# Gated linear attention and a cosine-gated MLP on one core: pairs 0 and 1 take both parities' decays from TensorE, and every engine gets a new written order

## The chip, the cores and the metric

The kernel runs on one core of one Trainium2 chip. The metric is the device time of one execution in microseconds (us), the median of several. Engines are named as the profile names them: PE is TensorE's matmul, PEld its weight load, DVE VectorE, ACT ScalarE, POOL GpSimd, and SP SyncE, which here only issues DMAs. A line such as L479 is a line of the kernel file; the changed file is longer, so its lines have other numbers.

## The reference

```python
B, H, S, D = 4, 8, 768, 48
f = 1.0 / (1.0 + np.exp(-f_logit))
for t in range(S):
    state = f[:, :, t, :, None] * state + np.einsum('bhd,bhe->bhde', k[:, :, t], v[:, :, t])
    y[:, :, t] = np.einsum('bhd,bhde->bhe', q[:, :, t], state)
x = y.transpose(0, 2, 1, 3).reshape(B * S, H * D)      # 3072 x 384
h = x @ w_in                                           # 3072 x 2048
out = (h * np.cos(h)) @ w_out                          # 3072 x 384, float32
```

The recurrence runs along the sequence, for each of 32 (batch, head) pairs with its own 48x48 state; the MLP then takes all heads of a token together.

## The kernel before

**Tiling.** A *pair* is 256 tokens of one batch, two chunks (g = 0, 1) of 128 tokens with all eight heads; there are 12 pairs, three to a batch. In a pair a partition holds an even and an odd token (parity e = 0, 1). The MLP works on *units* of 256 tokens, unit m on pair m's result.

**Steps of pair n** (u = 0, 1 is a half of four heads; pairs 0 and 1 are loaded and decayed by halves, `cut`, the others whole):

- `f`, `k`, `q`, `v`: loads on SP's queue (L296), 384 KB each, 192 KB for a half. `w0.i`, `w1.i` (L282): four parts each of `w_in` and `w_out`, 768 KB a part, into slots of the pool `g`; `wc0.i`, `wc1.i` (L197) cast a part to bf16 on POOL or ACT.
- `ex`, `ln` (L329, L333, ACT): the softplus of -f_logit, which is minus the log of the gate. `ad` (L363, POOL) adds both parities. `cum` (L374, L380, PE): products with a triangular matrix sum the logs over the tokens. `eb`, `ei` (L391, L395, ACT): exp of minus and plus that sum, the tiles `b` and `bi`.
- `fx`, `fy` (L347, L344), `ka` (L351), `qa` (L341; L338 in cut pairs) bring the one parity from the other: k's even token is multiplied by the odd token's gate, q's by its inverse. `qm`, `km` (L404, POOL or DVE): q times `b` and k times `bi`.
- `tq`, `tk` turn q and k: on PE (L435) with a copy `qkt` out of PSUM in pairs 0 to 3, by a DMA transpose (L424) in pairs 4 to 11. `sc` (L456, PE) and `am` (L461, DVE): scores and their mask. `vb`, `vt` (L197): casts and copies of v.
- `ps` (L479, PE): the state's increment. `st` (L497, DVE) adds the carried state to it in PSUM, `sz` (L503, DVE) decays the sum. `y`, `yi` (L531, PE): the output from within the pair and from the carried state; `xe` (L197) copies it out as the MLP's input.

**Steps of unit m**: eight `h` (L579, PE, six matmuls of 256 columns each), four `co` (L584, ACT, cosine), four `g` (L561, DVE), then for each of its two blocks of 128 tokens (numbered 0 to 23) four `o` (L595, PE, four matmuls of 384 columns), `ot` (L197) and the store `out` (L606). Part i of `w_out` is read by the steps `o*.i`.

**Order.** The text `ORDER` lists every step with its engine and its slots (`w0.1:Y0` is step w0.1 on SP, slot 0; T is PE, S ACT, V DVE, G POOL). It is all that sets each engine's instruction order; an engine takes its instructions strictly one behind the other, and a wait holds up all behind it. `zf` are fillers: products of zeros (L264, 512 columns) that nobody reads, placed where PE would wait. Each core fetches its instructions from memory by DMA as well: the profile counts them as queues of kind "instruction".

## Time and profile before

| | us |
|---|---|
| median of 3 runs (181.22 to 182.77) | 181.72 |
| span of the profiled execution, first to last instruction | 179.3 |
| PE busy in it | 171.0 (95%) |
| of that the 50 recorded fillers | 14.8 |
| DVE / ACT / POOL busy | 137.8 / 131.3 / 109.2 |
| the three DMA kinds: data loads and stores, share of 16 engines | 81.4% |

The profile gives no time of its own for the profiled execution beside its span. The 2.4 us between span and median lie around the span, before the first and behind the last instruction. A row of the timeline reads: start, duration, engine, line, operation, what it writes and reads, sizes, count, and in brackets the engine's idle time ahead of it with what ended it. In the table of stages the columns behind each stretch are its length, the busy time of PE, PEld, DVE, ACT and POOL, TensorE's granted clock, the DMA engines' busy share (over 1 where packets overlap) and GB/s.

### The profile page before, as it was taken

What the parts mean: (1) busy time and instruction counts of PE and PEld (TensorE: products, weight loads), DVE (VectorE), ACT (ScalarE), POOL (GpSimd) and SP (SyncE); (2) the same over time, 40 slices, a digit from 0 to 9 for tenths busy, and PEclk for the clock granted to TensorE, in tenths of its full rate; (3) what the DMA queues carried; (4) which work ended last, traced back from release to release, by engine and by line L of the source; (5) the groups of instructions that cost most, each with busy time, mean ns of one, the idle gap of its engine ahead of it and who ended that gap; (6) DMA issues with size and microseconds to landing.
All of it is one profiled execution on the core that took longest, in us unless ns stands there. A gap on an engine that the chain in (4) does not pass through costs nothing.

```text
span 179.3 us, 5727 instructions
## 1 busy us (share of the span) xinstructions
PE 171.0 (95%) x2412; PEld 122.9 (69%) x2414; DVE 137.8 (77%) x206; ACT 131.3 (73%) x185; POOL 109.2 (61%) x139
## 2 busy tenths in 40 slices
PE   7998899999999999999999998999999999999992
PEld 2453568876578866778668885668877766867761
DVE  6379998998894989969899887768689996385330
ACT  3899878886999998988999979858973702364410
POOL 7498699976979998789977295827992000000000
PEclk9999999999999999999999999999999999999999
DMA  6999999999999799999999999959045900004013
GB/s 156 262 261 287 356 324 315 306 274 328 257 257 236 168 190 180 282 277 198 249 203 262 226 254 207 234 131 268 4 106 121 148 0 4 4 0 176 0 50 129
DMA packets 74394, 34.46 MB, mean 192 GB/s; under 512 B 67456, under 2 KB 72832, under 8 KB 74368
## 3 DMA queue, kind: packets, MB, share of 16 engines
q1 hardware_dynamic: 73696, 33.79, 81.4%
q8 instruction: 19, 0.31, 0.8%
q10 hardware_dynamic: 672, 0.30, 0.6%
q14 instruction: 7, 0.06, 0.1%
HBM read 25.17 MB, written 4.72 MB: 167 GB/s over the span
## 4 chain that ended last, share of the span: by engine, by line
PE 69%; DMA 10%; POOL 7%; SPq 5%; DVE 5%; issue 3%; ACT 0%; POOLq 0%; DVEq 0%; ACTq 0%
PE ps L595 29%; PE ps L579 29%; DMA q<-in_q_dram 7%; SPq L296 5%; PE ps L531 4%; DMA qkt<-qk 3%; PE ps L456 3%; POOL qk L404 3%; PE ps L479 1%; POOL sp L363 1%; PE ps L435 1%; DVE qk L404 1%; POOL vt L197 1%; DVE sz L503 1%; PE ps L374 1%
## 5 line engine op out<-in xcount | busy, mean ns | idle before, releaser
L561 DVE TENSOR_TENSOR g<-ps,co 128x1024 bf16<-128x1024 f32 x48 | 57.7, 1221 | 15.3 <-ACT co L584 11.3
L595 PE MATMUL ps<-w_out_bf,g 128*128 128x384 bf16 x384 | 68.4, 326 | 0.0
L579 PE MATMUL ps<-x,w_in_bf 128*128 128x256 bf16 x576 | 66.7, 273 | 0.4 <-issue 0.4
L584 ACT ACTIVATE co<-ps,halfpi 128x1024 bf16<-128x1024 f32 x48 | 52.6, 1115 | 17.7 <-PE ps L579 14.4
L579 PEld LDWEIGHTS <-w_in_bf 128*128 128x128 bf16 x576 | 55.8, 98 | 9.2 <-issue 0.6
L595 PEld LDWEIGHTS <-g 128*128 128x128 bf16 x384 | 36.0, 98 | 21.5
L461 DVE TENSOR_TENSOR am<-ps,pmask 128x1024 bf16<-128x1024 f32 x24 | 28.7, 1215 | 3.6 <-PE ps L456 3.5
L404 POOL TENSOR_TENSOR qk<-q,b 128x384 bf16<-128x384 f32 x22 | 21.9, 1002 | 2.6 <-DVE q L338 1.7
L404 POOL TENSOR_TENSOR qk<-k,bi 128x384 bf16<-128x384 f32 x22 | 21.9, 1007 | 1.6 <-ACT bi L391 1.1
L197 POOL COPY vt<-vb 64x384 bf16<-64x384 bf16 x31 | 15.9, 514 | 1.4
L264 PE MATMUL ps<-zero 128*128 128x512 bf16 x50 | 14.8, 435 | 1.3 <-DVE zero L203 1.2
L503 DVE TENSOR_TENSOR sz<-ps,b 64x192 bf16<-64x192 f32 x40 | 14.2, 354 | 1.9 <-PE ps L479 0.9
L351 POOL TENSOR_TENSOR k<-k,f 128x384 f32<-128x384 f32 (+1 forms) x13 | 11.7, 904 | 6.2 <-DMA k<-in_k_dram 2.9
L197 DVE COPY ot<-ps 128x384 f32<-128x384 f32 (+1 forms) x17 | 8.7, 519 | 8.5 <-PE ps L595 6.0
L341 POOL TENSOR_TENSOR q<-f,q 128x384 f32<-128x384 f32 x10 | 10.0, 999 | 8.1 <-DMA q<-in_q_dram 8.1
L363 POOL TENSOR_TENSOR sp<-ls 128x384 bf16<-128x384 f32 x10 | 10.3, 1029 | 4.4 <-issue 2.2
L497 DVE TENSOR_TENSOR ps<-ps,sz 64x192 f32<-64x192 f32 x32 | 11.7, 366 | 1.4 <-PE ps L479 0.3
L329 ACT ACTIVATE f<-f 128x768 f32<-128x768 f32 (+1 forms) x14 | 10.4, 748 | 2.7 <-DMA f<-in_f_logit_dram 2.5
L197 ACT CAST x<-ps 128x384 bf16<-128x384 f32 x12 | 5.5, 479 | 8.6 <-PE ps L531 8.6
L197 ACT COPY ot<-ps 128x384 f32<-128x384 f32 (+1 forms) x9 | 4.1, 455 | 8.9 <-PE ps L595 8.9
L456 PE MATMUL ps<-qkt 48*64 48x128 bf16 (+1 forms) x320 | 8.6, 219 | 1.9 <-DVE qkt L197 1.0
L264 PEld LDWEIGHTS <-zero 128*128 128x128 bf16 x52 | 5.1, 108 | 6.9 <-issue 2.5
(61 smaller groups left out, 166.2 us busy)
## 6 DMA issues: line engine op xcount, KB each, us to landing
v<-in_v_dram SPq DMA_DIRECT2D x12, 384.0 KB, 6.1
out_dram<-ot SPq DMA_DIRECT2D x22, 192.0 KB, 2.8
f<-in_f_logit_dram SPq DMA_DIRECT2D x10, 384.0 KB, 5.6
k<-in_k_dram SPq DMA_DIRECT2D x10, 384.0 KB, 6.1
q<-in_q_dram SPq DMA_DIRECT2D x10, 384.0 KB, 6.4
g<-in_moe_w_in_dram SPq DMA_DIRECT2D x4, 768.0 KB, 7.5
g<-in_moe_w_out_dram SPq DMA_DIRECT2D x4, 768.0 KB, 7.2
k<-in_k_dram SPq DMA_DIRECT2D x4, 192.0 KB, 5.0
```

Source lines behind the costliest of these rows:

```text
L197: (nc.scalar.copy if e == "ACT" else eng(e).tensor_copy)(out=o, in_=i)
L264: G.step(f"zf{i}", ("PE",), lambda e, dump=dump: nc.tensor.matmul(dump.ap, lhsT=zero[:, 0:128], rhs=zero, start=True, stop=True), writes=[ ...
L351: eng(e).tensor_mul(out=w.ap[:, :, 0, :], in0=w.ap[:, :, 0, :], in1=t.ap[:, :, 0, :])
L363: G.step(f"ad{n}", ("POOL",), lambda e: eng(e).tensor_add(out=sp.ap[:, 0, :, 0:D], in0=soft.ap[:, :, 0, :], in1=soft.ap[:, :, 1, :]), read ...
L404: G.step(f"{nm}{n}.{u}", ("POOL", "DVE") if cut else ("POOL",), lambda e, u=u, j=j, src=src, dec=dec: eng(e).tensor_mul(out=qkp[u][j].ap[: ...
L456: nc.tensor.matmul(o[t0:t1, r, 2 * a + g, :].rearrange("p (e n) -> p e n", e=2), lhsT=wide[s, t0 // 64, :] if turned else wide[s].rearrang ...
L461: G.step(f"am{n}.{u}", ("DVE",), lambda e, u=u, sc=sc: nc.vector.tensor_mul(out=am[u].ap.rearrange("p r b n -> p (r b) n"), in0=sc.ap.rear ...
L503: eng(e).tensor_mul(out=new.ap[s, :, r, :].rearrange("p (u a) n -> p u a n", u=2), in0=view()[s].rearrange("p (u a) n -> p u a n", u=2), i ...
L561: nc.vector.tensor_mul(out=o.rearrange("p b (n e) -> p b n e", e=2), in0=ph.ap.rearrange("p (b e n) -> p b n e", e=2, n=64), in1=co.ap.rea ...
L579: nc.tensor.matmul(ph.ap[:, i * T:(i + 1) * T].rearrange("p (g t) -> p g t", t=C), lhsT=w_in_bf[:, kk, f0:f0 + 128], rhs=xa[:, :, kk, :], ...
L584: G.step(f"co{m}.{j}", ("ACT",), lambda e, ph=ph, co=co: nc.scalar.activation(out=co.ap, in_=ph.ap, func=AF.Sin, bias=halfpi), reads=[ph], ...
L595: nc.tensor.matmul(po.ap[:, 0:DM], lhsT=gT.ap[:, j, i * C:(i + 1) * C], rhs=w_out_bf[:, j, :], start=(po.first and j == 4 * s), stop=(po.f ...
```

## The change

In pairs 0 and 1 `cum` now makes one sum for each parity: a step has four products of 192 columns instead of two, three with the triangle that includes its own token and one with the strict one. `eb` and `ei` are twice as wide and go to new tiles `bb` and `bj`; `qm` and `km` take them for both parities at once. So `fx`, `qa` and `ka` of pairs 0 and 1 go. In pair 1 (`CARRY_PE`) the carried state is added by two products with the identity for each chunk (`si1.0`, `si1.1`, PE) behind the `ps` steps, and the four `st1` steps on DVE go. Fillers drop from 52 to 28. `ORDER` is new from end to end. The code for pairs in `VLIE` is not used, as `VLIE` is empty; it is left out here.

```diff
+CARRY_PE = (1,)
-ZEROS = 52
+ZEROS = 28
...
+    bbS = slots("bb", [128, 2, 2 * HB + 4], F32)
+    bjS = slots("bj", [128, 2, 2 * HB], F32)
...
-        sp, bt, bi = Val(spS), Val(bS), Val(biS)
+        sp, bt, bi = Val(spS), Val(bbS if cut else bS), Val(bjS if cut else biS)
...
+            if cut:
+                continue
             G.step(f"fx{n}{u}", ("ACT",), ...
...
+        W = HB * len(xe)
...
-            for x in xe:
-                nc.tensor.matmul(o[:, :, 0:HB], lhsT=incl,
-                                 rhs=w[:, x, :, 0:D].rearrange("p (u h) d -> p u h d", u=un),
-                                 start=(x == 0), stop=False)
+            for z in xe:
+                for x in xe:
+                    nc.tensor.matmul(o[:, :, HB * z:HB * z + HB], lhsT=strict if x > z and cut else incl,
+                                     rhs=w[:, x, :, 0:D].rearrange("p (u h) d -> p u h d", u=un),
+                                     start=(z == 0 and x == 0), stop=False)
...
-            if S0 is not None:
+            if S0 is not None and n in CARRY_PE:
+                def add(e, g=g, S0=S0):
+                    for r in range(2):
+                        nc.tensor.matmul(ps[g].ap[:, 0:HB].rearrange("p (a n) -> p a n", n=D), lhsT=ident,
+                                         rhs=S0.ap[:, :, r, :], start=(ps[g].first and r == 0),
+                                         stop=(ps[g].final and r == 1))
+                G.step(f"si{n}.{g}", ("PE",), add, reads=[S0] + both, writes=[ps[g]], sums=True)
+            elif S0 is not None:
...
-zvt.2:V zsp.2:V f0.1:Y0 zqk.2:G zsp.0:G f0.0:S ex0.1:S ln0.1:S2 f1.0:Y2 ex0.0:S fx0.1:S ln0.0:S
+f1.1:Y2 f0.1:S1 zf0:T5 v0:Y0 f0.0:S zf1:T0 q0.0:Y1 zqk.2:G k1.1:Y1 zqk.0:G zvt.2:G k0.0:Y2 ex1.1:S
```

**Three places in the order.** First the loads on SP behind the halves of q1, before: the four parts of `w_in` (`moe_w_in`, in the order 1, 0, 3, 2), pair 3's k and q, the parts 2, 0, 1, 3 of `w_out`, pair 2's q and k, pair 3's v.

```order
L282 DMA g_0_143<-in_moe_w_in_dram 128x3x512
L282 DMA g_1_144<-in_moe_w_in_dram 128x3x512
L296 DMA k_2_99<-in_k_dram 128x8x96
L282 DMA g_4_147<-in_moe_w_in_dram 128x3x512
L282 DMA g_0_143<-in_moe_w_in_dram 128x3x512
L296 DMA q_2_102<-in_q_dram 128x8x96
L282 DMA g_1_144<-in_moe_w_out_dram 128x4x384
L282 DMA g_4_147<-in_moe_w_out_dram 128x4x384
L296 DMA q_1_101<-in_q_dram 128x8x96
L296 DMA k_0_97<-in_k_dram 128x8x96
L296 DMA v_2_105<-in_v_dram 128x8x96
L282 DMA g_0_143<-in_moe_w_out_dram 128x4x384
```

And now the same stretch, with the parts of `w_in` in the order 1, 0, 2, 3 and pair 2's k and q apart:

```order
L295 DMA g_0_148<-in_moe_w_in_dram 128x3x512
L295 DMA g_3_151<-in_moe_w_in_dram 128x3x512
L295 DMA g_1_149<-in_moe_w_in_dram 128x3x512
L309 DMA k_2_100<-in_k_dram 128x8x96
L295 DMA g_2_150<-in_moe_w_in_dram 128x3x512
L309 DMA q_2_103<-in_q_dram 128x8x96
L295 DMA g_4_152<-in_moe_w_out_dram 128x4x384
L309 DMA k_1_99<-in_k_dram 128x8x96
L295 DMA g_3_151<-in_moe_w_out_dram 128x4x384
L309 DMA q_1_102<-in_q_dram 128x8x96
L309 DMA v_2_106<-in_v_dram 128x8x96
L295 DMA g_2_150<-in_moe_w_out_dram 128x4x384
```

No part of `w_in` goes to a slot that an earlier part holds any more (slot 0 stood twice before). Behind this the last part of `w_out`, which before stood ahead of pair 2's v, now stands behind it, as the last load ahead of pair 4's. 

Second, POOL from the first cast of `w_in` to the first of `w_out`, before (L351, L341, L404 are pair 3's `ka`, `qa` and its `km` and `qm`):

```order
L197 CAST w_in_bf<-g_143 128x3x512
L197 CAST w_in_bf<-g_144 128x3x512
L351 TENSOR_TENSOR k_99<-k_99,f_94 128x8x48
L404 TENSOR_TENSOR qk_119<-k_99,bi_115 128x8x48
L197 CAST w_in_bf<-g_147 128x3x512
L197 CAST w_in_bf<-g_143 128x3x512
L404 TENSOR_TENSOR qk_119<-k_99,bi_115 128x8x48
L341 TENSOR_TENSOR q_102<-f_94,q_102 128x8x48
L404 TENSOR_TENSOR qk_119<-q_102,b_112 128x8x48
L197 CAST w_out_bf<-g_144 128x1536
```

Now (L360, L350, L416 are the same three kinds):

```order
L196 CAST w_in_bf<-g_148 128x3x512
L196 COPY vt_130<-vb_122 64x8x48
L196 CAST w_in_bf<-g_149 128x3x512
L360 TENSOR_TENSOR k_100<-k_100,f_96 128x8x48
L416 TENSOR_TENSOR qk_120<-k_100,bi_115 128x8x48
L196 CAST w_in_bf<-g_150 128x3x512
L350 TENSOR_TENSOR q_103<-f_96,q_103 128x8x48
L416 TENSOR_TENSOR qk_120<-q_103,b_113 128x8x48
L416 TENSOR_TENSOR qk_120<-k_100,bi_115 128x8x48
L416 TENSOR_TENSOR qk_120<-q_103,b_113 128x8x48
L196 CAST w_out_bf<-g_152 128x1536
```

One cast of `w_in` has gone to ACT, and all four `qm` and `km` of pair 3 now stand ahead of the first cast of `w_out`, where three did.

Third, PE's start. Before, eleven fillers stood ahead of the first `cum`; now two do (each product has a weight load of its own ahead of it):

```order
L277 LDWEIGHTS zero
L277 MATMUL ps_165<-zero 128x512
L277 LDWEIGHTS zero
L277 MATMUL ps_163<-zero 128x512
L386 LDWEIGHTS incl
L386 MATMUL ps_164<-sp_109,incl 128x192
L386 LDWEIGHTS strict
L386 MATMUL ps_164<-sp_109,strict 128x192
L386 LDWEIGHTS incl
L386 MATMUL ps_164<-sp_109,incl 128x192
L386 LDWEIGHTS incl
L386 MATMUL ps_164<-sp_109,incl 128x192
```

L386 is `cum` of pair 1's second half, whose logits are now loaded first. In the text of `ORDER` the start-up on PE reads so (without slots): two fillers, `cum1.1`, four fillers, `cum0.0`, four, `cum0.1`, two, `tk0.0`, and on to `si1.0`, `tk1.0`, `yi0`, `y0`, `tq1.0`, `cum3`, `tq1.1`, a filler, `sc1.0`, `yi1`, `sc1.1`, `si1.1`, and then the first `h`. Its end now reads `o22.1`, `o23.1`, `o21.2`, `o21.0`, where before `o23.2` was last: the last store is now the whole of block 21 (192 KB, ACT's copy, SP's queue), and was before a half of block 23 (96 KB).

252 lines of the change are left out of this document (145 added, 107 removed).

## The prediction

> **What bounds the kernel now.** I read the table of stages first, then PE's timeline, then the loads.
>
> ```profile
> span 179.3 us, 5727 instructions
> ...
> q8 instruction: 19, 0.31, 0.8%
> ```
>
> ```profile
> 1.19 4.88 PE L264 MATMUL ps<-zero 128*128 128x512 bf16 x11 [1.19 <-DVE zero L203]
> ...
> 7.09 3.21 PE L264 MATMUL ps<-zero 128*128 128x512 bf16 x14
> ...
> 24.92 1.47 PE L579 MATMUL ps<-x,w_in_bf 128*128 128x256 bf16 x12
> ```
>
> PE is the bound, but in two different ways. Up to 24.92 us, where the first `h` starts, much of its work is fillers: there it waits for pairs 0 and 1. From there on it has work that counts, almost without a break. The list of all that PE waited for names only two waits over 0.3 us behind that point:
>
> ```profile
> 78.07 2.12 PE L579 MATMUL ps<-x,w_in_bf 128*128 128x256 bf16 x18 [0.38 <-issue]
> ...
> 111.72 0.42 PE L456 MATMUL ps<-qkt 48*64 48x128 bf16 x16 [0.64 <-DMA qkt<-qk]
> ```
>
> So 24.92 to the last product at 176 us is 151 us of work that the change leaves as it is: the same 96 `h`, 96 `o` and pairs 2 to 11. A gain can come from an earlier first `h`, from these 1.0 us of waits, from fewer changes between long and short matmuls, and from the tail. But the loads pace the start-up as well:
>
> ```profile
> 12.00:15.00 3.00, 2.33 (x34) 1.53 (x34) 2.89 (x7) 2.89 (x6) 2.91 (x7) 1.00 1.28 261
> ...
> 18.00:21.00 3.00, 2.19 (x84) 1.52 (x86) 2.80 (x6) 2.35 (x5) 1.64 (x2) 1.00 1.04 380
> ...
> 24.00:27.00 3.00, 3.00 (x69) 2.15 (x68) 2.57 (x4) 2.55 (x4) 2.92 (x4) 1.00 0.88 299
> ...
> 42.00:45.00 3.00, 3.00 (x60) 2.12 (x58) 2.57 (x6) 2.12 (x3) 1.63 (x3) 1.00 1.15 298
> ```
>
> The last column but one is the DMA engines' busy share: 1 or more all the way, except 0.88 from 24 to 27 us. What lands by a given time is then set by how many bytes stand ahead of it. The change loads the same bytes.
>
> **The edits beside the order.** With their prices from rows of before:
>
> ```profile
> L404 POOL TENSOR_TENSOR qk<-q,b 128x384 bf16<-128x384 f32 x22 | 21.9, 1002 | 2.6 <-DVE q L338 1.7
> L497 DVE TENSOR_TENSOR ps<-ps,sz 64x192 f32<-64x192 f32 x32 | 11.7, 366 | 1.4 <-PE ps L479 0.3
> ...
> L363 POOL TENSOR_TENSOR sp<-ls 128x384 bf16<-128x384 f32 x10 | 10.3, 1029 | 4.4 <-issue 2.2
> ```
>
> ```profile
> 5.43 0.35 ACT L347 ACTIVATE f<-sp 128x192 f32<-128x192 bf16 x1
> ...
> 7.26 0.33 ACT L391 ACTIVATE bi<-ps 128x192 f32<-128x192 f32 x1 [0.68 <-PE ps L380]
> ...
> 9.18 0.59 POOL L351 TENSOR_TENSOR k<-k,f 128x192 f32<-128x192 f32 x1
> ...
> 10.14 0.33 PE L374 MATMUL ps<-sp,incl 128*128 128x192 bf16 x2
> 10.56 0.38 DVE L338 SCALAR_TENSOR_TENSOR q<-f,q 128x192 f32<-128x192 f32 x1 [0.20 <-DMA q<-in_q_dram]
> ...
> 16.01 0.49 ACT L395 ACTIVATE bi<-ps 128x384 f32<-128x384 f32 x1 [0.26 <-PE ps L380]
> ```
>
> ACT loses four `fx` (4 x 0.35 = 1.4) and its eight exps grow from 0.33 to 0.49 (8 x 0.16 = 1.3): even. POOL loses three `ka` (1.8). DVE loses four `qa` (1.5), one `ka` and four `st1` (4 x 0.37 = 1.5). PE gains eight products of 192 columns (8 x 0.16 = 1.3) and the four of `si`, which the trace does not show; by the 0.16 they are 0.6, and between 0.2 (half of L374's, were they back to back) and 1.2 (a wait for `ps` each time). PE loses 24 fillers. Nearly all of that lies ahead of the first `h`, beside the loads, so it counts only through when `h` starts and what stands ready behind it.
>
> **When the first `h` starts.** PE reaches it behind `sc1.1`, which hangs on POOL's `qm1.1`, which stands behind pair 3's `ad3`, which needs the load f3:
>
> ```profile
> 16.91 0.84 ACT L329 ACTIVATE f<-f 128x768 f32<-128x768 f32 x1
> 17.79 0.84 ACT L333 ACTIVATE ls<-f 128x768 f32<-128x768 f32 x1
> ...
> 22.31 0.67 DVE L197 COPY qkt<-ps 128x1024 bf16<-128x1024 bf16 x1
> ...
> 23.72 0.40 PE L456 MATMUL ps<-qkt 48*128 48x128 bf16 x8
> ```
>
> With f3 there at 16.5 as before: `ex3` 0.84, three exps that now stand between (at 0.40 from start to start, 1.2), `ln3` 0.84, `ad3` 1.03, `qm1.1` 1.0, four transposes 0.4, the copy 0.67, `yi1` 0.35, `sc1.1` 0.40, and 0.5 for ten hand-overs: 16.5 + 7.2 = **23.7**, 1.2 earlier. Ends: 22.7 (f3 a us earlier) and 24.9, where it stands. For the late end: until 7 us fillers took 4.88 / 11 = 0.44 us and later 3.21 / 14 = 0.23; the four ahead of `cum0.1` at the slow rate put ACT's chain back by about a us.
>
> **What is late next.** Units 0 and 1 and pairs 2 and 3 fill PE until the first `h2`, here:
>
> ```profile
> 50.34 0.63 PE L531 MATMUL ps<-am,vt 128*32 128x128 bf16 x32
> ...
> 51.85 0.34 PE L374 MATMUL ps<-sp,incl 128*128 128x384 bf16 x1
> ...
> 52.77 0.33 PE L374 MATMUL ps<-sp,incl 128*128 128x384 bf16 x1
> ...
> 53.04 9.33 PE L579 MATMUL ps<-x,w_in_bf 128*128 128x256 bf16 x84
> ```
>
> ```profile
> 44.65 1.46 POOL L197 CAST w_out_bf<-g 128x1536 bf16<-128x1536 f32 x1 [1.30 <-DMA g<-in_moe_w_out_dram]
> 46.06 0.82 POOL L197 CAST vb<-v 128x768 bf16<-128x768 f32 x1
> ...
> 168.05 7.96 PE L595 MATMUL ps<-w_out_bf,g 128*128 128x384 bf16 x48
> ```
>
> Before, the last part of `w_out` came at 44.6 and pair 2's v by 46.06, one behind the other. The new order puts that part behind v: it lands when v did. The only slack in the queue is the dip at 24 to 27 us, SP being held by the load that wanted slot 0 again; the new slots free it: (1.04 - 0.88) x 3 / 1.04 = 0.46. So 45.6 for the last part, its cast until 47.1, and behind it on PE, four `o` (7.96 / 12 = 0.66 each, 2.65), a `cum` 0.27 (52.77 to 53.04), the `y` block 1.51 (50.34 to 51.85), a `cum` 0.27 and some 0.2 of changes: first `h2` at 52.0, a gain of 1.0 and no more, however early `h0` was.
>
> POOL gives nearly the same. Before, pair 3's q was there at about 30.4 (issued at 23.98, and the median q takes 6.4 to land):
>
> ```profile
> 23.98 1.48 SPq L296 DMA_DIRECT2D q<-in_q_dram  x1
> ...
> 36.85 2.11 PE L595 MATMUL ps<-w_out_bf,g 128*128 128x384 bf16 x12
> ```
>
> The new POOL order then has `qa3`, three `qm`/`km` (4 x 1.0) and the 1.46 of the first `w_out` cast: 35.9, with hand-overs 36.2, where PE before began `o` at 36.85. The sixteen `h` of units 0 and 1 (9.33 / 84 x 6 = 0.67 each, 10.7) and `y1` from 23.7 end at about 35, ahead of that, so about half of the 1.2 us is given back in a wait there. The like then happens at each of the loads up to the last part of `w_out`. I take `h2` at 52.3, a gain of **0.7**, since a single slip of POOL or DVE on the way costs directly; ends 1.5 (PE alone sets it) and -0.3 (start-up late, part late).
>
> **Behind `h2`** both orders hold the same PE work and the same number of changes between long and short matmuls (38 each, counted in the order). Both waits shown, 1.0 together, lie here. The one at 111.72 is a transpose's landing. In the new order its `sc8` stands behind four more `o` (2.6 us of PE work), but SP has one input, one store and one transpose more ahead of it (at the 261 to 298 GB/s of the stages above 1.4 for 384 KB, 0.7 for 192 KB, and by its 256 KB 0.9 for a transpose: 3.0). That is about a draw. The other ended with nothing that the profile shows ("issue"), I think with an instruction that had not been fetched yet. I take half of the 1.0 as gained: **0.5**; ends 1.0 and -1.5.
>
> Here a rule bears on it. The row of q8 says 19 fetches of 16 KB. The Trainium skill, "Runtime: NRT & Kernel Launch", section "Instruction fetch mechanics", says that a block is 256 instructions and that crossing to the next is "mostly hidden"; by it an order made with regard to fetches gains nothing, and the sum would be 0.2 worse. The 0.38 at 78.07 is the only sign against it, and bounds it.
>
> **The tail.**
>
> ```profile
> 170.20 0.48 ACT L197 COPY ot<-ps 128x384 f32<-128x384 f32 x1 [0.48 <-PE ps L595]
> ...
> 176.05 0.32 ACT L197 COPY ot<-ps 128x192 f32<-128x192 f32 x1 [4.07 <-PE ps L595]
> 176.40 0.36 DVE L197 COPY ot<-ps 128x192 f32<-128x192 f32 x1 [2.27 <-ACT ot L197]
> ```
>
> ```profile
> out_dram<-ot SPq DMA_DIRECT2D x22, 192.0 KB, 2.8
> out_dram<-ot ACTq DMA_DIRECT2D x1, 96.0 KB, 1.6
> ```
>
> Before: PE's end, two half copies in turn (0.71), a store of 96 KB (1.6). Now one whole copy (0.48), a store of 192 KB: 2.8 in the median among other loads, less here with the queues empty. -0.23 + 0.3 to 1.2: I take +0.35.
>
> **Sum.** -0.7 - 0.5 + 0.35 = -0.85: span 178.45, and with the 2.4 around it 180.85; predicted **180.9**. One per cent, 1.8 us, is about what a measurement of this kernel can tell from no change, so this is "the same", on the fast side of it.
>
> **Rivals.** *The start-up's gain is kept whole* (24 in 100). If POOL and the loads have more slack than I see, `h2` gains the 1.2, and 0.4 of changes between matmul kinds (counted in the order, six fewer from the first `h` to `h2`, some 0.07 each: the eight `o` from 44.56 run 1.40 against 1.33 in the long run of 48), the waits go (1.0), the tail costs 0.1. For it: PE had no wait at all from 25 to 70 us. Against: the full queue. -2.5: 179.2.
>
> ```profile
> 44.56 1.46 PE L595 MATMUL ps<-w_out_bf,g 128*128 128x384 bf16 x8
> 45.96 0.62 PE L456 MATMUL ps<-qkt 48*128 48x128 bf16 x16
> ```
>
> *The order gives nothing* (13): the waits go elsewhere, the draw at `sc8` is lost by 0.8 and the start-up late. 181.7.
>
> *PE at the slow rate, slower than before* (13). Fillers at 0.44 and then 0.23 us show that PE runs at half speed until it has been busy for some time, here from 1.19 to between 5.4 and 7.1, 4.2 to 5.9 us. The new order idles PE from 2.0 to 5.1 (only two fillers ahead of `cum1.1`, which needs a load and two ACT steps) and has 24 fewer fillers after. If it is still, or again, slow at the first `h`, half of such a stretch is lost: 2.1 to 2.9. It decides where the waits between fillers in 13 to 24 us add up to several us without work. Against it: before, a wait of 0.93 and some of 0.4 did no harm, and I count PE three quarters busy there. 180.9 + 2.4 = 183.3. The Trainium skill, "TensorE: Matmul & The Clock Gate", section "Part 1: The HAM clock gate", says the clock is halved by default and after an idle window of about 3.4 us, and freed after a busy one. The trace agrees with the first warm-up; that an idle stretch halves it again no run here shows, and the profile's clock row reads 9 throughout.
>
> **Numbers.** Forecast 50, whole gain 24, nothing 13, slow PE 13. Faster by over 1%: 0.24; within: 0.63; slower: 0.13. The range 179.0 to 183.0 takes the whole gain's 179.2, the sum of the bad ends (-0.3 and -1.5 with the tail's +1.0 make +2.8 on 181.7; it goes to half of that) and most of the slow case, and leaves out what goes beyond on both sides.
>
> **What will show it.** Right: first `h` between 22.7 and 24.9; a PE wait or a late POOL cast ahead of the first `o` near 36; the last `w_out` cast at 45.5 to 47.5 and `h2` at 51.5 to 53; no wait over 0.5 behind it. Wrong: fillers of 0.4 us behind 12 us; `h2` ahead of 51.3, which would mean that the loads do not pace it; or transposes that land late at pairs 8 and 9.

## The result, and the profile after

The changed kernel takes **180.37 us** in the median of ten runs (179.59 to 181.57). Ten runs of the kernel before, taken with them, have a median of 182.43 (181.22 to 182.78): the ratio is 0.990, with a 95% interval of 0.988 to 0.993. A second set gave 180.48 against 181.79, 0.993 (0.990 to 0.996). So the change makes the kernel faster, by 0.7 to 1.0 per cent. That is just inside what the prediction called "the same", though the interval of the first set reaches beyond it. The forecast was 180.9.

The page of the changed kernel, first its span and its fetches of instructions:

```profile
span 178.5 us, 5663 instructions
...
q8 instruction: 19, 0.31, 0.8%
```

The span is 0.8 shorter than the 179.3 of before; PE still makes 19 fetches. PE's timeline answers to the rows shown of before (L277 are fillers, L386 `cum`, L634 `h`, L451 transposes, L650 `o`, L572 `y`):

```profile
1.19 1.03 PE L277 MATMUL ps<-zero 128*128 128x512 bf16 x2 [1.19 <-DVE zero L202]
5.27 0.32 PE L386 MATMUL ps<-sp,incl 128*128 128x192 bf16 x1 [3.05 <-ACT sp L346]
...
6.02 1.87 PE L277 MATMUL ps<-zero 128*128 128x512 bf16 x4
...
8.81 1.02 PE L277 MATMUL ps<-zero 128*128 128x512 bf16 x4
...
23.52 1.47 PE L634 MATMUL ps<-x,w_in_bf 128*128 128x256 bf16 x12
...
34.66 1.06 PE L451 MATMUL ps<-ident,qk 128*128 128x128 bf16 x16
...
36.06 2.76 PE L650 MATMUL ps<-w_out_bf,g 128*128 128x384 bf16 x16 [0.34 <-POOL w_out_bf L196]
...
52.33 3.93 PE L634 MATMUL ps<-x,w_in_bf 128*128 128x256 bf16 x34 [0.17 <-DVE x L196]
```

The first `h` is at 23.52 (24.92 before), the first `o` at 36.06 behind a wait for POOL's cast (36.85), the first `h2` at 52.33 (53.04). Of the 1.40 us at the start 0.71 is left at `h2`. The fillers at 6.02 take 1.87 / 4 = 0.47 each and those at 8.81 0.26: PE comes to its full rate later than before (the trace lists the full granted clock from 8.68 us on, that of before from 7.18), and is there long before the first `h`. What a still later one costs shows the second profile of this kernel, in the last of the experiments.

Behind `h2`, the two waits over 0.3 us, and PE's last `o`:

```profile
95.75 0.64 PE L472 MATMUL ps<-qkt 48*64 48x128 bf16 x32 [0.33 <-DMA qkt<-qk]
...
100.08 0.63 PE L572 MATMUL ps<-am,vt 128*32 128x128 bf16 x32 [0.52 <-POOL vt L196]
...
166.01 9.26 PE L650 MATMUL ps<-w_out_bf,g 128*128 128x384 bf16 x56
```

```profile
175.31 0.48 ACT L196 COPY ot<-ps 128x384 f32<-128x384 f32 x1 [1.24 <-PE ps L650]
```

The two waits of before (0.38 and 0.64) are gone, and two others of 0.33 and 0.52 have come, both in pair 7's steps. PE's last product ends at 166.01 + 9.26 = 175.27, before at 176.01: the 0.7 of `h2` is still there at the end, with nothing gained or lost in between, in 123 us. From there to the end of the span it is 3.2 us, as before (179.3 - 176.01 = 3.3).

### The profile page after: what moved, and what is told of

It is laid out like the page before. It is cut to its first block, busy times and chain, and to the rows that moved or that the text cites. A ratio compares the mean times of both kernels' runs of the same rounds, so it can differ in the third digit from the quotient of the medians.

```text
span 178.5 us, 5663 instructions
## 1 busy us (share of the span) xinstructions
PE 168.0 (94%) x2402; PEld 121.4 (68%) x2402; DVE 134.1 (75%) x201; ACT 129.1 (72%) x179; POOL 106.6 (60%) x134
## 4 chain that ended last, share of the span: by engine, by line
PE 65%; POOL 14%; DMA 10%; SPq 4%; ACT 3%; issue 2%; DVE 1%; POOLq 0%
PE ps L650 31%; PE ps L634 23%; DMA g<-in_moe_w_in_dram 6%; POOL qk L416 6%; PE ps L572 4%; DMA v<-in_v_dram 3%; PE ps L472 3%; POOL q L350 2%; DMA f<-in_f_logit_dram 2%; SPq L309 2%; POOL k L360 2%; PE ps L386 2%; POOL w_in_bf L196 1%; PE ps L512 1%; POOL vt L196 1%
## 5 line engine op out<-in xcount | busy, mean ns | idle before, releaser
L650 PE MATMUL ps<-w_out_bf,g 128*128 128x384 bf16 x384 | 67.3, 326 | 0.3 <-POOL w_out_bf L196 0.3
L634 PE MATMUL ps<-x,w_in_bf 128*128 128x256 bf16 x576 | 66.3, 273 | 0.2 <-DVE x L196 0.2
L634 PEld LDWEIGHTS <-w_in_bf 128*128 128x128 bf16 x576 | 55.4, 98 | 8.6 <-issue 0.4
L650 PEld LDWEIGHTS <-g 128*128 128x128 bf16 x384 | 36.3, 98 | 22.8 <-issue 0.5
L416 POOL TENSOR_TENSOR qk<-k,bi 128x384 bf16<-128x384 f32 x20 | 19.8, 997 | 0.6
L416 POOL TENSOR_TENSOR qk<-q,b 128x384 bf16<-128x384 f32 x20 | 19.7, 999 | 0.7
L544 DVE TENSOR_TENSOR sz<-ps,b 64x192 bf16<-64x192 f32 x32 | 11.3, 354 | 1.3 <-PE ps L512 0.4
L196 DVE COPY ot<-ps 128x384 f32<-128x384 f32 (+1 forms) x16 | 8.1, 514 | 5.5 <-PE ps L650 5.5
L360 POOL TENSOR_TENSOR k<-k,f 128x384 f32<-128x384 f32 x10 | 10.0, 999 | 3.3 <-ACT ot L196 2.9
L538 DVE TENSOR_TENSOR ps<-ps,sz 64x192 f32<-64x192 f32 x28 | 10.2, 366 | 1.9 <-PE ps L512 0.9
L196 ACT COPY vt<-vb 64x384 bf16<-64x384 bf16 x16 | 8.1, 508 | 4.2 <-POOL vb L196 3.9
L350 POOL TENSOR_TENSOR q<-f,q 128x384 f32<-128x384 f32 x10 | 10.0, 996 | 1.2 <-ACT f L353 1.1
L277 PE MATMUL ps<-zero 128*128 128x512 bf16 x28 | 9.4, 431 | 1.2 <-DVE zero L202 1.2
L196 POOL CAST vb<-v 128x768 bf16<-128x768 f32 x8 | 6.6, 822 | 5.1 <-DMA v<-in_v_dram 5.1
```

Source lines behind the costliest of these rows:

```text
L196: (nc.scalar.copy if e == "ACT" else eng(e).tensor_copy)(out=o, in_=i)
L350: eng(e).tensor_mul(out=w.ap[:, :, 0, :], in0=t.ap[:, :, 1, :], in1=w.ap[:, :, 0, :])
L360: eng(e).tensor_mul(out=w.ap[:, :, 0, :], in0=w.ap[:, :, 0, :], in1=t.ap[:, :, 0, :])
L416: G.step(f"{nm}{n}.{u}", ("POOL", "DVE") if cut else ("POOL",), lambda e, u=u, j=j, src=src, dec=dec: eng(e).tensor_mul(out=qkp[u][j].ap[: ...
L544: eng(e).tensor_mul(out=new.ap[s, :, r, :].rearrange("p (u a) n -> p u a n", u=2), in0=view()[s].rearrange("p (u a) n -> p u a n", u=2), i ...
L634: nc.tensor.matmul(ph.ap[:, i * T:(i + 1) * T].rearrange("p (g t) -> p g t", t=C), lhsT=w_in_bf[:, kk, f0:f0 + 128], rhs=xa[:, :, kk, :], ...
```

## Experiments

All runs in one table. The ratio is to runs of the kernel before on the same chip; those had medians of 181.8 to 182.4. The columns behind it are from the profile of one run each; that of edits_old_again is the longest of its twelve runs (183.19).

| run | median us | ratio (95%) | first `h` | first `h2` | last PE product | span |
|---|---|---|---|---|---|---|
| before, the profile shown above | | | 24.92 | 53.04 | 176.01 | 179.3 |
| before_again | 182.13 | 1.000 (0.996 to 1.004) | 25.79 | 53.90 | 177.26 | 180.5 |
| changed kernel | 180.37 | 0.990 (0.988 to 0.993) | 23.52 | 52.33 | 175.27 | 178.5 |
| after_again | 180.48 | 0.993 (0.990 to 0.996) | 24.93 | 53.12 | 175.22 | 178.5 |
| edits_old_order | 180.43 | 0.992 (0.989 to 0.995) | 24.16 | 52.53 | 174.92 | 178.5 |
| edits_old_again | 180.74 | 0.994 (0.991 to 0.998) | 24.28 | 52.98 | 177.83 | 181.4 |
| sums_only | 180.98 | 0.997 (0.994 to 1.000) | 24.19 | 52.44 | 175.91 | 179.5 |
| after_fixed | 181.22 | 0.999 (0.996 to 1.002) | 24.38 | 53.95 | 176.50 | 179.7 |
| after_no_fillers | 182.32 | 1.006 (1.003 to 1.009) | 26.09 | 54.28 | 176.80 | 180.0 |
| edits_28 | 181.10 | 0.997 (0.994 to 1.000) | 22.92 | 52.37 | 175.56 | 179.1 |
| edits_28_moves | 180.74 | 0.994 (0.992 to 0.997) | 23.32 | 51.65 | 176.16 | 179.8 |
| edits_36_moves | 180.35 | 0.991 (0.989 to 0.994) | 23.40 | 51.73 | 174.62 | 178.2 |
| new_start | 193.62 | 1.063 (1.059 to 1.068) | 24.17 | 52.36 | 188.89 | 192.5 |
| new_rest | 186.69 | 1.024 (1.019 to 1.029) | 24.25 | 53.60 | 181.38 | 184.6 |

### The kernel before, once more

No edit.

> The kernel before, unchanged, profiled once more. Its timed runs lie between 181.2 and 182.8, and the first profile (span 179.3) may be one of the short ones. Theory A (the prediction's): the profile repeats the first within 0.3 us at the first h (24.92), the first h2 (53.04) and the last product (176.0), and the medians differ for what lies around the span. Theory B: the kernel has waits behind h2 that come and go; then this profile, if its span is near 180.4, shows h2 near 53.0 again and 0.8 to 1.2 us more of waits on PE behind it than the 1.0 us of the first.

The spans of the 33 runs of this kernel in this set lie between 178.7 and 181.9, each 1.7 to 1.95 us under its time; the 2.4 around the span that the prediction worked with is not there. By that the first profile (179.3) would belong to a run of 181.0 to 181.3, one of the shortest. So neither theory's account of the difference was right: it lies within the span, and most of it ahead of the first `h`. This profile's rows on PE and, for the way to them, on DVE (L338 is `qa1`, L404 `qm1.1`, L497 `st1`, L503 `sz1`, L197 the copy `qkt1.1`):

```profile
25.79 0.38 PE L579 MATMUL ps<-x,w_in_bf 128*128 128x256 bf16 x2
...
53.90 0.81 PE L579 MATMUL ps<-x,w_in_bf 128*128 128x256 bf16 x6
```

```profile
19.49 0.94 DVE L338 SCALAR_TENSOR_TENSOR q<-f,q 128x192 f32<-128x192 f32 x1 [0.36 <-DMA q<-in_q_dram]
20.53 1.16 DVE L404 TENSOR_TENSOR qk<-q,b 128x384 bf16<-128x384 f32 x1
21.73 0.77 DVE L497 TENSOR_TENSOR ps<-ps,sz 64x192 f32<-64x192 f32 x2
22.53 0.72 DVE L503 TENSOR_TENSOR sz<-ps,b 64x192 bf16<-64x192 f32 x2
23.18 0.67 DVE L197 COPY qkt<-ps 128x1024 bf16<-128x1024 bf16 x1
```

Here q1.1, pair 1's second half of q, lands at 19.47, and from there DVE is busy almost without a break until `qkt1.1`, behind which stand `sc1.1` and the first `h`. In the first profile it had landed at 18.90, and `qa1.1` took 0.36 instead of 0.94 (more on this in the last section). Of the 1.25 us by which PE ends later here, 0.87 is there at the first `h`. The rest came behind it: the wait for the transpose ahead of `sc8.0` is 0.84 instead of 0.64, and PE's stop without a cause in the profile 0.56 instead of 0.38.

### The edits without the new order

`ORDER` is that of the kernel before, without `fx`, `qa`, `ka` of pairs 0 and 1; the two `si1` stand behind `ps1.1` and behind the decays of chunk 0.

```diff
-ZEROS = 28
+ZEROS = 52
-f1.1:Y2 f0.1:S1 zf0:T5 v0:Y0 f0.0:S zf1:T0 q0.0:Y1 zqk.2:G k1.1:Y1 zqk.0:G zvt.2:G k0.0:Y2 ex1.1:S
+zvt.2:V zsp.2:V f0.1:Y0 zqk.2:G zsp.0:G f0.0:S ex0.1:S ln0.1:S2 f1.0:Y2 ex0.0:S ln0.0:S zf0:T0 zf1:T0
...
+sz0.11:V q1.1:Y qm1.1:V ln3:S0 fx3:S vt0.2:G km1.1:G ps1.1:T si1.0:T y0:T3,5 yi0:T xe0.0:S0 vt1.3:S
```

> All edits of the change (sums per parity, no fx, qa, ka in pairs 0 and 1, carried state of pair 1 by identity products), but in the order of before with its 52 fillers: what the edits alone are worth. Theory A: the first h stays near 24.9, since it hangs on pair 3's chain, and the time stays within 0.4 us of before. Theory B (waits behind h2 carry the difference): the same, within 0.4, unless the moved instructions shift a wait. A third, that the edits carry the gain: 1 to 2 us faster than before.

Theories A and B missed, and the third held: 1.4 us faster than before. The edits alone bring what the whole change brings, as far as intervals of some 0.4 per cent can tell. The same stretch on DVE (L414 is `qm1.1`, L542 `sz1`, L194 the copies):

```profile
19.12 0.72 DVE L414 TENSOR_TENSOR qk<-q,bb 128x384 bf16<-128x384 f32 x1 [0.85 <-DMA q<-in_q_dram]
19.87 0.72 DVE L542 TENSOR_TENSOR sz<-ps,bb 64x192 bf16<-64x192 f32 x2
21.36 0.69 DVE L194 COPY qkt<-ps 128x1024 bf16<-128x1024 bf16 x1 [0.76 <-PE ps L449]
```

```profile
24.16 1.47 PE L632 MATMUL ps<-x,w_in_bf 128*128 128x256 bf16 x12
...
52.53 2.23 PE L632 MATMUL ps<-x,w_in_bf 128*128 128x256 bf16 x19
```

q1.1 lands at 19.03 and `qm1.1` starts at once, the `qa1.1` ahead of it being gone; it takes 0.72 where it took 1.16; and DVE, rid of `st1`, now waits 0.76 for PE's transposes. From q1.1's landing to the first `h` it is 5.1 us here, and 25.79 - 19.47 = 6.3 and 24.92 - 18.90 = 6.0 in the two profiles of before. f3 lands at 17.61 here, 1.1 later than in the first profile of before (16.55), and does not matter: in the old order the way to the first `h` goes by q1.1, not by f3.

The end of that way is made of fillers. With 52 of them, four stand directly ahead of the first `h`; in the first profile of before:

```profile
24.05 1.04 PE L264 MATMUL ps<-zero 128*128 128x512 bf16 x4
```

From their start to the first `h` it is 0.87 us (24.05 to 24.92, and 23.29 to 24.16 in edits_old_order). The changed kernel has only `si1.1` in that place, 0.35. So of the 1.40 by which its first `h` comes earlier, 0.88 is there at `sc1.1` (22.84 for 23.72), and 0.52 is the four fillers less `si1.1`. The first `h` in edits_28 below, the edits in the old order with 24 fillers fewer, comes at 22.92.

> All edits in the order of before with 52 fillers, again, on the chip of the run above. Theory C: 180.3 to 180.8, a stop of PE of 0.4 to 0.6 us at its 2234th instruction again, 2.76 us behind the start of a fetch.

180.74, on another chip: again as fast as the changed kernel beside it (180.48), within the intervals. The expected stop did not come in this run's profile: PE reached the place later, 3.65 us behind the start of the fetch (see the last section).

### The sums alone

The run above, with the four `st1` steps back in place of the two `si1`.

```diff
-CARRY_PE = (1,)
+CARRY_PE = ()
...
-ps1.1:T si1.0:T y0:T3,5
+ps1.1:T y0:T3,5
...
+fy3:S st1.01:V st1.00:V sz1.01:V1 zf41:T0 zf42:T0 zf43:T0 tq1.1:T0 sz1.00:V qm1.0:G tq1.0:T qkt1.0:S2
```

> The sums per parity (no fx, qa, ka in pairs 0 and 1) in the order of before with its 52 fillers, but pair 1's carried state still added by the four st1 steps on DVE. In the run with all edits in this order the first h came at 24.2 (before: 24.9 and 25.8), although f3 landed later; its chain there goes from q1.1's landing over DVE (qm1.1, the decays sz1, the copy qkt1.1) to sc1.1. Theory C: what counts are DVE steps behind q1.1's landing; the two st1 (0.75) stand there, the qa1.1 (0.4 to 0.9) is gone: first h near 24.9, 0.5 to 0.8 us slower than all edits, 181.0 to 181.2. Rival: the sums alone bring it, the carried state does nothing: within 0.3 of 180.4. Second rival: the carried state brings all: within 0.3 of before.

```profile
24.19 1.47 PE L633 MATMUL ps<-x,w_in_bf 128*128 128x256 bf16 x12
```

The first `h` does not move (24.19 against 24.16): the two `st1` fall into DVE's 0.76 of waiting, so theory C is wrong on them. The carried state on PE does nothing for the start; the time, 180.98, lies between before and all edits, and its interval touches both, so whether `si1` is worth anything at all stays open. By these rows what brings the earlier start in the old order is the missing `qa1.1` (0.36 to 0.94) and the shorter `qm1.1` (0.44); neither was tried alone.

### Half an order from each

The changed kernel's order up to its first `h2` with the rest of before, and the other way round; where a value's slot was still in use at the seam, it got a free one. The seam of new_start, and of new_rest:

```diff
-fx5:S ka4:G xe2.1:V fy4:S cum5:T7 sz3.10:V1 ei5:S0 h2.11:T2 sz3.11:V ka5:G out2:Y eb5:S2
+f6:Y2 km4.0:G eb5:S0 km4.1:G tq4.1:Y0 tq4.0:Y1 km5.1:G2 h2.10:T2 h2.11:T co2.1:S0 h2.00:T4 h2.01:T
```

```diff
-km4.1:G tq4.1:Y0 tq4.0:Y1 km5.1:G2 ot1:V1 xe2.0:V1 xe2.1:V h2.10:T2 h2.11:T co2.1:S0 h2.00:T0 h2.01:T
+km5.1:G2 ot1:V1 xe2.0:V1 xe2.1:V ot3:V3 fy5:S f9:Y1 h2.11:T2 out2:Y xe3.1:V3 h2.10:T xe3.0:V h2.21:T6
```

> The changed kernel's order up to its first h2, and from there on the order of before (tail included). Theory A: it holds the start's 0.7 us (h2 at 52.3) and the waits of before behind it: 0.5 to 0.9 us faster than before. Theory B: 0.7 from the start but slower than the changed kernel by 1 us or more, that is 0.3 to 0.9 faster than before, with waits of 1.5 us or more behind h2.

> The edits in the order of before up to the first h2 (with its 52 fillers), from there on the changed kernel's order. Theory A: h2 near 53.0 as before, the rest no better than before's: within 0.3 us of before, 0.5 to 0.9 slower than the changed kernel. Theory B: the new rest is free of the waits that come and go: 1.0 to 1.5 us faster than before.

As tests of the two theories both are lost: the halves don't fit, and the time goes into waits that neither kernel has. new_start gave two things all the same. Its first `h2`, at 52.36, repeats the changed kernel's 52.33. And its waits show what PE does after an idle stretch (L382 `cum`, L568 `yi` and `y`, L630 `h`):

```profile
58.85 5.40 PE L630 MATMUL ps<-x,w_in_bf 128*128 128x256 bf16 x48 [2.40 <-DVE g L612]
...
75.88 0.50 PE L382 MATMUL ps<-sp,incl 128*128 128x384 bf16 x1 [3.23 <-ACT ot L192]
...
76.39 0.83 PE L568 MATMUL ps<-qkt,sz 128*32 128x128 bf16 x24
77.00 1.07 PE L568 MATMUL ps<-am,vt 128*32 128x128 bf16 x32
...
82.76 0.52 PE L568 MATMUL ps<-qkt,sz 128*32 128x128 bf16 x24
83.11 0.62 PE L568 MATMUL ps<-am,vt 128*32 128x128 bf16 x32
```

```profile
75.00:80.00 5.00, 4.12 (x82) 2.89 (x83) 1.78 (x2) 4.23 (x8) 2.15 (x3) 0.50 1.01 263
```

Behind 3.23 us without work the same `yi` and `y` take 0.83 and 1.07 that take 0.52 and 0.62 later, and the granted clock is 0.50 in that stage. Behind 2.40 us the 48 products run at 5.40 / 48 = 0.11 us, the full rate. (In the 3.23 the clock had fallen after 2.14 already; see the last section.)

### No fillers at all

```diff
-ZEROS = 28
+ZEROS = 0
```

> The changed kernel without any filler. If PE runs at half rate until it has been busy for some us, and again after an idle stretch, then short products run at half rate through the start and the first h at 0.22 us a product instead of 0.11 for 3 to 5 us: first h 0.5 to 1.5 late and the time 2 to 4 us longer than the changed kernel's 180.4. If the fillers don't matter by 28: within 0.5 of it.

```profile
24.00 0.61 PE L466 MATMUL ps<-qkt 48*128 48x128 bf16 x8
...
25.59 0.40 PE L466 MATMUL ps<-qkt 48*128 48x128 bf16 x8
...
26.09 1.47 PE L628 MATMUL ps<-x,w_in_bf 128*128 128x256 bf16 x12
```

PE runs at the slow rate all the way to 24 us (`sc1.0` takes 0.61, `sc1.1` behind it 0.40), and the first `h` comes at 26.09, 1.2 to 2.6 later than in the two profiles with 28 fillers; the `h` themselves are at full rate. 182.32 is 1.9 above the changed kernel's 180.37, which is from another set; by the ratios to before, 1.006 against 0.990 and 0.993, it is 1.3 to 1.6 per cent, 2.3 to 2.9 us, as expected. The granted clock of the profile reads 0.997 for this run, though the trace lists the full clock only from 25.49 us on: the slow rate of a start doesn't show in that mean.

### Fewer fillers in the old order, and five moved steps

edits_28 is edits_old_order without 24 of its fillers. edits_28_moves then moves single steps on PE:

```diff
-sc2.0:T0 sc2.1:T6 o2.3:T o1.3:T o2.1:T ps2.0:T0 ps2.1:T o0.3:T o1.1:T
+sc2.0:T0 sc2.1:T6 o2.1:T o1.1:T o2.3:T o1.3:T ps2.0:T0 ps2.1:T o0.3:T
...
-cum5:T5 h2.10:T2 h2.11:T
+h2.10:T2 h2.11:T cum5:T5
...
-y4:T sc5.0:T0 o6.2:T
+y4:T o6.2:T sc5.0:T0
...
-sc8.0:T6 o11.1:T
+o11.1:T sc8.0:T6
```

> All edits in the order of before, but with 28 fillers: 24 of the 41 behind the first cum are left out. So every later instruction of PE stands 48 places earlier in its program. In three traces PE stops for 0.4 to 0.6 us at its 2234th or 2236th instruction from the start, whatever step stands there, 2.76 us after an instruction fetch begins. Theory D (that wait is for the fetch, and its place goes by the count of instructions): the stop goes, since the 56 short products of y5, which run through 112 instructions in 0.9 us, then stand elsewhere in the block; 0.4 to 0.7 us faster than all edits with 52 fillers (180.4), so 179.7 to 180.0. Rival: the stop belongs to the step (ps6, h4.3) and stays; no gain. Second rival (the prediction's slow PE): with fewer fillers PE idles into the slow rate, fillers behind 12 us at 0.43 us, and it gets 1 to 3 us slower.

The stop is gone, but the time is no better. The first `h` is early (22.92), and PE then stands at the cast of the last part of `w_out`, as that stands at the part's landing. PE, and POOL's row for the cast:

```profile
45.85 2.11 PE L646 MATMUL ps<-w_out_bf,g 128*128 128x384 bf16 x12 [1.08 <-POOL w_out_bf L192]
```

```profile
44.34 1.47 POOL L192 CAST w_out_bf<-g 128x1536 bf16<-128x1536 f32 x1 [1.31 <-DMA g<-in_moe_w_out_dram]
```

The first `h` is 1.24 us ahead of edits_old_order: `sc1.1` by 0.43, and the rest is the four fillers behind it. Of the 1.24, 0.16 is left at `h2` (52.37 against 52.53). This is the mechanism by which the prediction had the start's gain given back, in the kernel where it really happens.

> All edits in the order of before with 28 fillers, and five moves on PE alone: two o that read an earlier part of w_out stand ahead of the two that read the last one (in the run with 28 fillers PE waited 1.08 for its cast, which hung on its landing at 44.3), cum5 stands behind the first two h2 (it hangs on f5's landing), one o ahead of sc5.0 (0.96, for DVE) and one ahead of sc8.0 (0.65, for a transpose). Theory F (the loads and DVE pace single steps, and PE has other work for these waits): first h at 23.0 to 23.9, h2 near 51.5 instead of 52.3, the three waits gone: 1.2 to 2.0 us faster than without the moves (181.1), 179.1 to 179.9 and 2 to 2.7 faster than before. Rival: the moved work is paid again by the next wait on the same landing: within 0.5 of 181.1.

At `h2` it came nearly as theory F has it: 51.65. From there the rival: two waits that were not there before, for DVE's `g` behind `h2.31` and for its `ot` ahead of `sc9.1`.

```profile
PE ps L468 <- DVE ot L192: 0.9, 1, 0.9
PE ps L630 <- DVE g L612: 0.8, 1, 0.8
```

And in this execution PE fell to the slow rate after a wait of 1.75:

```profile
10.48 0.24 PE L382 MATMUL ps<-sp,incl 128*128 128x192 bf16 x1 [1.75 <-ACT sp L342]
```

```profile
12.00:18.00 6.00, 5.51 (x47) 3.56 (x45) 5.77 (x11) 5.11 (x10) 4.64 (x9) 0.50 1.25 278
```

Five of its twelve runs have a mean clock of 0.979 to 0.981; their times are 0.7 above the mean of the others (181.2 and 180.5). edits_28 has the same wait of 1.75 and the same fillers; its profile and nine of its twelve runs read 0.996 or more. The last section says what makes the difference.

### Both new waits moved away as well

Eight fillers back where PE idled between 8.7 and 18 us, `cum5` one `h` earlier, `sc9.1` behind four steps:

```diff
-ZEROS = 28
+ZEROS = 36
...
-h2.10:T2 h2.11:T cum5:T5
+h2.10:T2 cum5:T5 h2.11:T
...
-sc9.0:T6 sc9.1:T4 ps9.1:T1,3 ps9.0:T o10.0:T o10.1:T
+sc9.0:T6 ps9.1:T1,3 ps9.0:T o10.0:T o10.1:T sc9.1:T4
```

> The run with 28 fillers and moved steps, with eight fillers put back where PE idles between 8.7 and 18 us (in its trace PE ran at half rate from 12 to 18.3 us after a wait of 1.75), cum5 one h earlier (it had held ACT's cosine back, so that h2.30 waited 0.8 for DVE), and sc9.1 behind four steps (it waited 1.0 for a copy on DVE). Theory F goes on: the clock stays at 0.996 or more in all runs, both waits go, h2 at 51.3 to 51.8, and the time is 0.7 to 1.5 us below 180.7: 179.2 to 180.0, faster than the changed kernel's 180.4. Rival (each wait that goes comes back on the next late thing, as DVE, ACT, the loads and PE all run close to the limit here): 180.2 to 180.7, no better than the changed kernel.

The list of PE's waits has nothing over 0.3 left behind the first `h`, the clock is 0.998 or more in all six runs, and PE ends at 174.62, the earliest of all. The time is 180.35, ratio 0.991: no better than the changed kernel. That list holds only waits that are long enough to be put down to something: from the first `h` to the last product it is 151.2 us here, no less than the 151.1 of before with its two waits. The rest must lie in waits too short for the list. And some of PE's gain is lost behind PE: from its last product to the end of the span it is 3.6 us here, and 3.6 in all profiles of the edits in the old order, against 3.2 to 3.3 in before and after, with the same last copies and stores as before. In these kernels POOL clears its semaphores at the end 0.26 to 0.3 us behind the last that PE does there, elsewhere within 0.04 of it. What holds POOL there is open.

### The changed kernel with its three waits taken away, and once more

```diff
-tk3.0:T0 tq3.0:T tq3.1:T6 tk3.1:T o2.2:T1 o1.2:T7 o0.2:T0
+tq3.1:T6 tk3.1:T o2.2:T1 o1.2:T7 tk3.0:T0 tq3.0:T o0.2:T0
...
-qm3.0:G wc1.2:G
+wc1.2:G qm3.0:G
...
-vt7.0:G vt7.1:G vb8:G0 vt8.2:G1
+vt7.0:G vt7.1:G vt7.3:G vb8:G0 vt8.2:G1
...
-tq7.0:Y0 out6:Y v8:Y2 tq7.1:Y3
+tq7.0:Y0 v8:Y2 tq7.1:Y3 out6:Y
```

> The changed kernel with the three waits of PE that its trace shows behind the first h taken away by moving single steps: the first cast of w_out goes ahead of pair 3's last qm on POOL (and two transposes of pair 3 behind two o on PE), pair 7's last vt goes ahead of pair 8's vb on POOL, and pair 7's second DMA transpose ahead of a store on SP. Theory E (each wait is paid in full at the end): 0.34 + 0.33 + 0.52, 1.0 to 1.2 us faster than the changed kernel: 179.2 to 179.4. Rival: something else is late right behind each of them, and less than 0.4 is left.

The three waits are gone, and the rival holds: `o3.2` now waits 0.78 for the copy of a transpose, `sc7.1` 0.46 for an `ot`, and with 181.22 it is slower: 0.999 (0.996 to 1.002) to before, against 0.990 and 0.993 for the changed kernel, is 0.6 to 0.9 per cent.

> The changed kernel once more, beside the edits in the old order on the same chip. Theory C (the edits bring the gain, the order nothing beyond it): within 0.4 us of the next run and 1.2 to 1.8 faster than before. Rival: the new order is worth 0.5 us or more by itself. Its first h should lie between 23.5 and 24.4, as in the three traces that share this start.

Its first `h`, 24.93, misses what was expected (23.5 to 24.4). The two profiles of the changed kernel are the clearest test of all. In this one the first `h` comes 1.41 us later, and there is no wait over 0.3 us from there on:

```profile
24.93 1.47 PE L634 MATMUL ps<-x,w_in_bf 128*128 128x256 bf16 x12
...
53.12 1.14 PE L634 MATMUL ps<-x,w_in_bf 128*128 128x256 bf16 x9 [0.17 <-DVE x L196]
...
100.03 0.63 PE L572 MATMUL ps<-am,vt 128*32 128x128 bf16 x32
...
165.96 9.26 PE L650 MATMUL ps<-w_out_bf,g 128*128 128x384 bf16 x56
```

`y7` starts at 100.03, in the first at 100.08; the last product ends at 175.22 and 175.27. 0.79 of the 1.41 is left at `h2`, nothing at `y7`. What holds `y7` is POOL, which stands at pair 8's v and has `vt7.3` behind it; here and in the first profile:

```profile
94.90 0.82 POOL L196 CAST vb<-v 128x768 bf16<-128x768 f32 x1 [1.36 <-PE ps L392]
...
99.47 0.50 POOL L196 COPY vt<-vb 64x384 bf16<-64x384 bf16 x1
```

```profile
94.97 0.82 POOL L196 CAST vb<-v 128x768 bf16<-128x768 f32 x1 [1.26 <-DMA v<-in_v_dram]
...
99.53 0.50 POOL L196 COPY vt<-vb 64x384 bf16<-64x384 bf16 x1
```

The cast is put down to PE in the one and to the load in the other; v8 landed at 94.75 and 94.82, right ahead of it in both. By these two profiles the start's gain is, in the new order, slack that POOL's queue and that load take up.

Why is the first `h` 1.41 later? Not for f3, which lands at 15.97 here and at 15.80 in the first profile. PE comes to its full rate later, and so do the four fillers ahead of `cum0.1` (1.02 in the first profile). Then ACT's exp of `cum0.1` comes later too; here, and the exp in the first profile:

```profile
9.06 1.87 PE L277 MATMUL ps<-zero 128*128 128x512 bf16 x4
...
11.70 0.49 ACT L403 ACTIVATE bj<-ps 128x384 f32<-128x384 f32 x1 [1.97 <-PE ps L392]
```

```profile
10.29 0.49 ACT L403 ACTIVATE bj<-ps 128x384 f32<-128x384 f32 x1 [0.81 <-PE ps L392]
```

From there on ACT is busy almost without a break, and `ex3` starts at 17.10 here, at 15.83 in the first profile. The four profiles with this start agree:

```
kernel             full clock from   the four fillers   that exp   first h   behind the exp
changed kernel                8.68               1.02      10.29     23.52            13.23
new_start                     9.93               1.52      10.87     24.17            13.30
after_fixed                  10.51               1.81      11.15     24.38            13.23
after_again                  11.67               1.87      11.70     24.93            13.23
```

So in the new order the first `h` goes by when PE reaches its full rate, with ACT's queue between. The nine profiles with the old start, eleven fillers ahead of the first `cum`, list the full clock from 4.05 to 7.18 us on; behind the new start, with two, it comes at 8.68 to 11.67, and the first `h` moves with it by 1.4 us.

## Why the prediction was right, and where it was not

**The first `h`** was to come at 23.7 (22.7 to 24.9): 23.52 and 24.93, and 24.17 and 24.38 in two more kernels with the same start. The steps named are the right ones for the new order: `ad3` ran on POOL from 18.85 to 19.86, `qm1.1` behind it to 21.15, then transposes, copy, `sc1.1`. What sets their time was named wrong. The sum starts with f3's landing, but f3 (15.80, 0.75 earlier than before) is there when ACT comes free for `ex3` at 15.79, and in after_again (15.97) ACT comes free only a us later. It is the prediction's late end that describes the other three profiles: slow fillers ahead of `cum0.1` put ACT's chain back by about a us. In the old order the way goes by q1.1. And the chain leaves out the four fillers ahead of the first `h` of before, 0.87 of the 1.2 that it has as gain, and the 0.35 of `si1.1` in the new one. That 23.7 is so near 23.52 is in part luck. That the edits count "only through when `h` starts" fits what they do in the old order, where the gain was there without the new one.

**Half of the start given back at the first `o`:** 36.06 for 36.2, with the wait for POOL's cast that was named. Of the 0.61 between the gains at first `h` (1.40) and first `o` (0.79), about 0.5 is that wait: the transposes ahead take 1.40 from their start to the first `o` here, and 0.90 in after_again, which doesn't wait (the row has only 0.34, as it counts from the modelled end of the products). Some 0.1 is work, two more groups of transposes that stand ahead of it now. Mechanism and size were right.

**The loads to the last part of `w_out`:** it landed at 44.65, a us earlier than the 45.6 worked out; the dip of the DMA engines at 24 to 27 us is gone, as expected (1.11, was 0.88). The cast still ended at 46.81, since POOL came to it only at 45.34. PE did not wait for it at all. From the first `o` to `h2` it is 16.27 us of PE's work, in before 16.19. So `h2` at 52.33, forecast 52.3, came out of a sum whose limiting step was not the limiting one here: that it agrees is luck. edits_28 shows the kernel in which the step limits.

**Behind `h2`**, 0.5 was to be gained, and in the first profile 0.0 was. Both old waits went; `sc8`, called a draw, was won. What the step missed is that a PE that comes earlier meets the next late thing: pair 7's `vt7.3` and transpose. In after_again, where PE comes later and doesn't wait, it is 0.9 (122.10 us from `h2` to the last product, in before 122.97).

**The tail** was forecast 0.35 longer and is as long as before: the whole last block's copy and store are done in the time of the two halves. The store of 192 KB took 1.85 us, the last half's in before 1.64: 0.21 more, where 0.3 to 1.2 was put, and the copy gives 0.23 back. This term was mis-sized, and it made up for the waits.

**The sum** was -0.85 on the span, and -0.8 came. That is luck in part: 0.5 behind `h2` did not come, and 0.35 at the tail was not lost. The other profile of before has a span 1.2 longer, too. The step from the span to the time was wrong: 2.4 around the span, where the runs of before have 1.7 to 1.95 and 17 of 19 of the changed kernel 1.8 to 1.9. The profile of before was, by that, of a short run, and against the medians the change gains 1.3 to 2.1, 0.7 to 1.0 per cent.

**The rivals.** PE was not slow at the first `h` in the changed kernel, but it was slow until 8.7 and 11.7 us in its two profiles, and that moved the first `h`. The rival's price was of the right size: without fillers 2.3 to 2.9 us, forecast 2.4 for half a stretch. That an idle stretch halves the clock again, which no run showed then, new_start, new_rest and edits_28_moves show. The whole gain kept did not come about either, and edits_36_moves suggests why: with no wait over 0.3 us left in the list it is no faster; DVE, POOL and the loads seem to stand right behind PE. On the fetches the prediction took a rule for the likelier side; the runs showed one stop of PE (below), worth 0.2 to 0.6 in the profiles that have it. The changed kernel doesn't have it in full, and edits_28, without 24 of the fillers, doesn't either, in the old order.

## What to carry to other kernels

Before a change of order is credited with a gain, run its edits in the old order: here they brought all of it that could be told. Look at what stands directly ahead of the first large matmul, fillers too: four of them held it up by 0.87 us. But see what fewer fillers do at the very start: with few, PE came to its full rate at 8.7 us in one execution and at 11.7 in another, and the first large matmul 1.4 us later. When an engine is 95% busy and three others and the loads run close behind it, removing its waits one by one moves them: a wait that is seen in one execution can be mere slack, which a second profile of the same kernel with another start shows at once. Take the time around the span from runs that list both.
